# Scaling and turning x of block 3 later, and building the turned output weights of the last two pairs later

## The chip, the cores and the metric

The kernel runs on one core of a Trainium2 chip. What counts is the device time of one execution in microseconds (us), as the median of several runs; three runs of the kernel before took 1274.93 to 1278.03 us. A core has five engines, each with its own queue of instructions in a fixed order: TensorE (PE, matmuls), VectorE (DVE), ScalarE (ACT), GpSimd (POOL) and SyncE (SP, which issues DMA transfers here). Engines wait for each other through semaphores only.

## The reference

Two batches of q, k, v with 6016 rows and 256 channels go through attention over channels, and the 12032 rows that come out go through a gated feed-forward network.

```
qn = q / (norm(q, axis=1) + 1e-06);  kn = k / (norm(k, axis=1) + 1e-06)
a = softmax(kn.transpose(0, 2, 1) @ qn / tau)        # 256 x 256 per batch
x = (v @ a).reshape(12032, 256)
xn = x / sqrt(mean(x * x, axis=-1) + 1e-06) * rms_g
g = xn @ w_gate;  val = xn @ w_val                    # 256 -> 1536
out = (g / (1 + exp(-g)) * val) @ w_out               # 1536 -> 256
```

All is float32. The kernel splits each operand into a high and a low part and adds three products, so that the result keeps its accuracy.

## The kernel before, in words

The first 130 us or so load q and k and add up the scores. The rest is the feed-forward network over blocks of up to 512 rows. A block j is walked in 12 steps f = 0 to 11, one per 128 of the 1536 hidden channels. Blocks 0 and 1 use a plain form (`emit_hidden`). From block 2 on, `emit_step` forms gate and value of a step by a scheme with seven products in place of eight, for which x of the block is kept in seven combinations (`xp`) and the weights in turned form (`s_hl`, made by `build_s`). From block 4 on, the pairs of steps in `PAIRS = (2, 3, 4)` use the same scheme for the output matmuls, with output weights turned by `build_so` (lines 598 to 620).

**A step.** `emit_step` works on three values of f at once: `now` begins products 5 and 1, `mid_` adds 3 and 6, `old` adds 7, 2 and 4. The four groups of PE instructions are therefore, in order: 7 and 2 of old, 3 and 6 of mid, 5 and 1 of now, then the first half of the output matmuls of a step five steps back, product 4 of old, and the second half. Products 1, 6, 7 and 4 share one half of a PSUM bank, `u[:, 1]`: ACT copies it away between them (line 771 after product 1, line 766 after product 6), and DVE adds it up after product 7 (line 759, then 760). PE may start product 3 only when line 771 is done, product 7 only when line 766 is done, and product 4 only when line 759 is done. For even f of old, ACT then applies Silu (lines 775 and 793); for odd f, DVE multiplies (lines 778 and 787) and the result is rounded on ACT (line 692) and its low part made on POOL (line 698). The buffers `t` of lines 766 and 771 are two, those of `u` three.

**What sets the order.** The kernel runs under a manual schedule: each engine's queue is filled in the order in which Python emits the instructions. Around the steps, two tables do this. `turn0` to `turn4`, `steady` and their `_mid` forms name per block and per f what is emitted within a step (`mid`, ahead of the output matmuls) or behind it; `extra`, filled by `at(j, f, go)`, names single pieces behind the step (j, f).

**x of a block.** `emit_x` makes v @ a in PSUM, `emit_x_squares` and `emit_rr` the norm of each row, `emit_xn` (line 476, ACT) scales half a block. `emit_xT_move` transposes 32 x 32 pieces on DVE (line 511) and, after the second half, issues 16 SBUF-to-SBUF copies on SP (line 520). `emit_xT_scale` multiplies by rms_g (line 530, ACT), `emit_xT_parts` forms the combinations on POOL (lines 541 and 546), `emit_xT_round` rounds them (line 558, ACT) and makes low parts (line 560, POOL). In block 2 this is done for block 3 by `turn2` and `turn2_mid`.

**A build of output weights.** `build_so(k, 0)` adds high and low part (line 602) and forms four combinations (line 612, four instructions), all on DVE; `build_so(k, 1)` rounds them on ACT (line 618, two); `build_so(k, 2)` makes low parts on DVE (line 620, two). They share one buffer, `wk`, with each other and with the output sums of a block: the evictions of block 3 (line 940, emitted after step 4 of block 4) can start only when the last build has been read. `move_v` (line 413, DVE) transposes v of a later block.

Of the kernel before, what the change touches and what calls it, by code (L numbers as in the profile page):

```python
# [19 lines left out]
def kernel(  # L20
# [62 lines left out]
    def f32(ap):  # L83
        return ap.bitcast(F32)
# [382 lines left out]
    def emit_xn(j, h, share=False):  # L467
        px, rr = xps.pop((j, h))
        for i, t in enumerate(half_tiles(j, h)):
            if share and i == 0:  # L470
                nc.vector.tensor_scalar(
                    out=xnt[j][:, t, :], in0=px[:, i, :], scalar1=rr[:, i:i + 1], scalar2=None,
                    op0=ALU.mult,
                )
                continue
            nc.scalar.activation(
                out=xnt[j][:, t, :], in_=px[:, i, :], func=AF.Copy, scale=rr[:, i:i + 1]
            )
# [26 lines left out]
    def emit_xT_move(j, c):  # L505

        n = blocks[j][2]
        if c == 0:
            moved[j] = xn_p.tile([P, KC, A, BT, S], F32, tag="moved", name=f"xw_{j}")
        w = moved[j]  # L510
        nc.vector.transpose(
            out=w[:, c, :, :n, :].rearrange("p i t s -> p t i s"),
            in_=xnt[j][:, :n, c * P:(c + 1) * P].rearrange("p t (i r) -> p t i r", r=S),
        )
        if c < KC - 1:
            return
        x = xn_p.tile([P, KC, BN], F32, tag="xn", name=f"xnT_{j}")
        for a in range(A):
            for i in range(A):
                nc.sync.dma_start(  # L520
                    out=x[S * i:S * (i + 1), :, a * n * S:(a + 1) * n * S],
                    in_=w[S * a:S * (a + 1), :, i, :n, :].rearrange("p c t s -> p c (t s)"),
                )
        moved[j] = x
# [73 lines left out]
    def build_so(k, piece):  # L598
        p = PAIRS[k]
        if piece == 0:  # L600
            t = s_tmp["so", k] = pool["wk"].tile([P, 4, 2 * P], F32, tag="wk", name=f"wo_{k}")
            nc.vector.tensor_tensor(
                out=t[:, :2], in0=f32(wo[0][:, 2 * p:2 * p + 2]), in1=f32(wo[1][:, 2 * p:2 * p + 2]),
                op=ALU.add,
            )
            a12, a22, a11, a21 = (t[:, i, e * P:(e + 1) * P] for i in range(2) for e in range(2))
            s1, s2, s3, s4 = (t[:, 2 + i, e * P:(e + 1) * P] for i in range(2) for e in range(2))
            for o, i0, i1, op in (
                (s1, a21, a22, ALU.add), (s2, s1, a11, ALU.subtract),
                (s3, a11, a21, ALU.subtract), (s4, a12, s2, ALU.subtract),  # L610
            ):
                nc.vector.tensor_tensor(out=o, in0=i0, in1=i1, op=op)
        else:
            t = s_tmp["so", k][:, 2:].rearrange("p i n -> p (i n)")
            src = (t[:, :3 * P], t[:, 3 * P:])
            hi, lo = ([x[:, k], w[:, 2 * p + 1, P:]] for x, w in zip(so_hl, wo))
            for o, x in zip(hi, src) if piece == 1 else ():
                nc.scalar.activation(out=o, in_=x, func=AF.Copy)
            for o, x, y in zip(lo, src, hi) if piece == 2 else ():
                nc.vector.tensor_tensor(out=o, in0=x, in1=f32(y), op=ALU.subtract)  # L620
# [341 lines left out]
    with tc.manual_schedule():  # L962
# [128 lines left out]
        def at(j, f, go):  # L1091
            extra.setdefault((j, f), []).append(go)
# [43 lines left out]
        for i in (2, 3, 0, 1):  # L1136
            for p in range(NP):
                j, f = divmod(NF + at_step[p][i], NF)
# [12 lines left out]
            )  # L1151

        at(STRA - 1, 6, new_so)
        for i, k, f in ((0, 0, 10), (1, 0, 11), (2, 0, 12), (0, 1, 12), (1, 1, 13), (2, 1, 14), (0, 2, 14), (1, 2, 15)):
            at(STRA - 1 + f // NF, f % NF, lambda k=k, i=i: build_so(k, i))

        at(3, 1, lambda: inverse_norms(1))
# [31 lines left out]
        def xn(h):  # L1189
            return lambda n: emit_xn(n, h)  # L1190

        def xm(c):
            return lambda n: emit_xT_move(n, c)
# [4 lines left out]
        def of(m, go):  # L1198

            def run(j):  # L1200
                n = j + m
                if m < 0 and n < WINO or n >= NB:
                    return
                go(n)
            return run

        v0, s0, v1, s1 = (of(2, go) for go in (vm(0), vs(0), vm(1), vs(1)))
        x0, q0, r0, n0, x1, q1, r1, n1 = (of(2, go(h)) for h in range(2) for go in (x, sq, rr, xn))
# [5 lines left out]
        after = lambda m, *gos: tuple(of(m, go) for go in gos)  # L1214
# [22 lines left out]
            5: (rest,),  # L1237
            6: (s1, store),
        }
        turn4_mid = {4: (lambda j: build_so(2, 2),), 6: (x0, q0, r0), 8: (x1, q1), 9: (n1,)}  # L1240
        turn3 = {
            3: (v0,),
            4: (c0, c1, scale, s0),
# [6 lines left out]
            11: (m0, m1),  # L1250
        }
        turn3_mid = {5: (parts,), 7: (x0, q0, r0), 9: (x1, q1), 11: (n1,)}
        turn2_mid = {**turn3_mid, 0: after(1, xn(1)), 5: ()}
        turn2 = {
            **turn3,
            0: after(1, xm(0), xm(1)),
            4: (s0,),
            5: (scale,),
            6: (parts, hi, v1),
# [36 lines left out]
        for i, (j, f) in enumerate(steps + [(None, None)] * 2):  # L1296
# [5 lines left out]
            k = min(j, 5) if j is not None else None  # L1302
# [56 lines left out]
```

## Time and profile before

| what | value |
|---|---|
| median of three runs | 1277.2 us (1274.93 to 1278.03) |
| profiled execution | 1276.13 us |
| its span, first to last instruction | 1274.3 us |
| busy: PE / DVE / ACT / POOL | 99% / 69% / 68% / 63% |
| share of the chain that ended last on PE | 91% |
| PE clock granted over the span | 0.996 of full speed |

The span is what the profiler's rows cover; 1.8 us of the execution lie around it. In the timelines below a row is one instruction, or several alike in a row with their count. It gives the start from the span's beginning, how long it took, the engine, the line, what it writes and reads and in which shape. A bracket at its end says how long the engine was idle in front of it, and what it waited for.

### The profile page before, as it was taken

Reading aid. Unit: us, or ns where it says so; the run is one execution under the profiler, and the core shown is the slowest. Engines: PE = TensorE matmul, PEld = TensorE weight load, DVE = VectorE, ACT = ScalarE, POOL = GpSimd, SP = SyncE. Lnnn points to the kernel's source line nnn. Section 1 sums busy time; section 2 is a strip of 40 time slices with the busy share of each in tenths; the row PEclk is TensorE's granted clock in tenths of the full one; section 3 lists DMA queues with packets and bytes.
Section 4 is the critical chain, followed back from the end, with each engine's and each line's share of the span. In section 5 each row is a group of like instructions: output and inputs, shape, how many; then the busy total and the mean of one; then the engine's idle time right before and its main releaser. Section 6 shows DMA issues by size and latency. Waiting matters only on the chain.

```text
span 1274.3 us, 25137 instructions
## 1 busy us (share of the span) xinstructions
PE 1259.3 (99%) x9225; PEld 1199.5 (94%) x9225; DVE 884.7 (69%) x1573; ACT 869.6 (68%) x1771; POOL 803.0 (63%) x639
## 2 busy tenths in 40 slices
PE   8899999999999999999999999999999999999998
PEld 7798988999999999999999999999999999999998
DVE  5789688658667657667766666676676676676664
ACT  5577556666777687677777767767767767777654
POOL 0120245765777777777776777777777777777652
PEclk9999999999999999999999999999999999999999
DMA  8879111120221211211212202202202202101101
GB/s 286 292 239 282 50 27 42 26 42 18 46 32 24 45 25 34 41 27 34 38 23 42 36 19 47 34 18 51 34 18 51 34 18 50 30 19 30 18 1 30
DMA packets 223964, 71.77 MB, mean 56 GB/s; under 512 B 186592, under 2 KB 215392, under 8 KB 223840
## 3 DMA queue, kind: packets, MB, share of 16 engines
q1 hardware_dynamic: 223008, 68.92, 23.6%
q8 instruction: 72, 1.18, 0.4%
q10 hardware_dynamic: 832, 1.25, 0.3%
q14 instruction: 52, 0.43, 0.1%
HBM read 46.40 MB, written 12.32 MB: 46 GB/s over the span
## 4 chain that ended last, share of the span: by engine, by line
PE 91%; DMA 3%; DVE 3%; SPq 1%; ACT 1%; issue 1%; POOL 0%; POOLq 0%; DVEq 0%; ACTq 0%
PE pu L730 44%; PE po L904 26%; PE pq L730 7%; PE px L435 5%; PE s L174 4%; DMA raw<-in_k_dram 2%; PE po L854 2%; PE pg L813 1%; PE pv L813 1%; DVE wk L587 1%; SPq L520 1%; DMA raw<-in_q_dram 1%; DVE acc L198 0%; DMA wraw<-in_moe_w_out_dram 0%; DVE zh L827 0%
## 5 line engine op out<-in xcount | busy, mean ns | idle before, releaser
L730 PE MATMUL pu<-xt,w 128*128 128x256 f32 (+1 forms) x2376 | 410.7, 281 | 0.4 <-DVE zv L759 0.3
L730 PE MATMUL pu<-xt,s 128*128 128x256 f32 (+1 forms) x2376 | 366.0, 280 | 0.8 <-ACT t L766 0.8
L730 PEld LDWEIGHTS pu<-xt,w 128*128 128x128 f32 x2376 | 347.2, 189 | 13.9 <-DVE zv L759 1.0
L730 PEld LDWEIGHTS pu<-xt,s 128*128 128x128 f32 x2376 | 326.9, 188 | 13.2 <-ACT t L766 1.0
L698 POOL TENSOR_TENSOR gy<-zg,gy 128x512 fp32r<-128x512 f32 (+1 forms) x131 | 182.2, 1391 | 149.6 <-ACT gy L692 85.5
L698 POOL TENSOR_TENSOR gx<-zg,gx 128x512 fp32r<-128x512 f32 (+2 forms) x131 | 200.8, 1533 | 87.3 <-ACT gx L692 85.1
L771 ACT ACTIVATE t<-pu 128x512 f32<-128x512 f32 (+1 forms) x264 | 157.0, 595 | 99.6 <-PE pu L730 83.4
L904 PE MATMUL po<-gx,w 128*128 128x256 f32 (+1 forms) x927 | 197.4, 331 | 0.0
L766 ACT ACTIVATE t<-pu 128x256 f32<-128x256 f32 (+1 forms) x264 | 100.1, 379 | 90.4 <-PE pu L730 87.8
L759 DVE TENSOR_TENSOR zv<-pu,t 128x512 f32<-128x512 f32 (+1 forms) x132 | 89.7, 679 | 102.8 <-ACT zg L793 76.6
L778 DVE TENSOR_TENSOR zg<-zg,zv 128x768 f32<-128x768 f32 (+1 forms) x132 | 148.9, 1128 | 14.4 <-ACT t L766 0.5
L692 ACT ACTIVATE gx<-zg 128x512 fp32r<-128x512 f32 (+2 forms) x132 | 95.1, 720 | 72.2 <-DVE zg L787 36.9
L684 DVE TENSOR_TENSOR zg<-zg 128x256 f32<-128x256 f32 x228 | 96.9, 425 | 67.8 <-POOL gx L698 61.9
L904 PEld LDWEIGHTS po<-gx,w 128*128 128x128 f32 x927 | 137.1, 188 | 6.1 <-ACT os L940 0.2
L730 PE MATMUL pq<-xt,w 128*128 128x256 f32 (+1 forms) x792 | 137.3, 281 | 0.0
L787 DVE TENSOR_TENSOR zg<-pu,zg 128x256 f32<-128x256 f32 (+1 forms) x132 | 55.6, 421 | 95.3 <-PE pu L730 94.1
L759 DVE TENSOR_TENSOR zg<-pu,t 128x512 f32<-128x512 f32 (+1 forms) x132 | 89.0, 674 | 44.3 <-PE pu L730 28.7
L904 PE MATMUL po<-gy,w 128*128 128x512 f32 x414 | 118.4, 394 | 0.0
L698 POOL TENSOR_TENSOR gz<-zg,gz 128x512 fp32r<-128x512 f32 x57 | 112.8, 1979 | 0.0
L730 PEld LDWEIGHTS pq<-xt,w 128*128 128x128 f32 x792 | 112.2, 188 | 0.0
L775 ACT ACTIVATE zg<-zg 128x768 f32<-128x768 f32 (+1 forms) x132 | 109.6, 831 | 0.0
L174 PE MATMUL s<-raw 128*128 128x256 f32 x376 | 89.6, 394 | 6.8 <-DMA raw<-in_k_dram 4.5
(146 smaller groups left out, 2041.1 us busy)
## 6 DMA issues: line engine op xcount, KB each, us to landing
v<-in_v_dram SPq DMA_DIRECT2D x84, 128.0 KB, 3.8
xnT<-xw SPq DMA_DIRECT2D x336, 32.0 KB, 1.9
out_dram<-ob SPq DMA_DIRECT2D x84, 128.0 KB, 3.3
raw<-in_q_dram SPq DMA_DIRECT2D x20, 512.0 KB, 5.9
raw<-in_k_dram SPq DMA_DIRECT2D x19, 512.0 KB, 6.8
wraw<-in_moe_w_gate_dram SPq DMA_DIRECT2D x12, 256.0 KB, 4.4
wraw<-in_moe_w_val_dram SPq DMA_DIRECT2D x12, 256.0 KB, 4.9
wraw<-in_moe_w_out_dram SPq DMA_DIRECT2D x12, 256.0 KB, 5.6
```

The source lines that it names most:

```text
L174: nc.tensor.matmul(out=s_ps[b][:, c, :], lhsT=r[:, 1, t, c * P:(c + 1) * P], rhs=r[:, 0, t, :], start=(t0 + t == 0 and c == 0), stop=(t0 + ...
L435: nc.tensor.matmul(out=px[:, i, :], lhsT=w[:, c, i * P:(i + 1) * P], rhs=x[:, c, :], start=(i == 0 and c == 0 and m == 0), stop=(c == KC - ...
L684: nc.vector.tensor_tensor(out=z[:, o], in0=z[:, i0], in1=z[:, i1], op=ALU.subtract)
L692: nc.scalar.activation(out=gh, in_=hh, func=AF.Copy)
L698: engine.tensor_tensor(out=gl, in0=hh, in1=f32(gh), op=ALU.subtract)
L730: nc.tensor.matmul(out=out, lhsT=wm[wi], rhs=xm[xi], start=(start and q == 0), stop=(q == 2), skip_group_check=True,)
L759: nc.vector.tensor_tensor(out=z[:, 1:], in0=u, in1=t[:, :2], op=ALU.add)
L766: nc.scalar.activation(out=mt[:, 0], in_=mu[:, 1], func=AF.Copy)
L771: nc.scalar.activation(out=nt[:, 1:], in_=nu, func=AF.Copy)
L775: nc.scalar.activation(out=zg[:, 1:], in_=zg[:, 1:], func=AF.Silu)
L778: nc.vector.tensor_tensor(out=zg[:, 1:], in0=zg[:, 1:], in1=z, op=ALU.mult)
L904: nc.tensor.matmul(out=acc[b][:, o:o + g.shape[-1]], lhsT=w, rhs=g, start=first, stop=True, skip_group_check=True,)
```

## The change

Five lines of the tables change. For block 3, the scaling of the second half of x (`xn(1)`) is emitted within step 1 of block 2 instead of step 0, and the two transposes with the copies (`xm(0)`, `xm(1)`) behind step 2 instead of step 0. The builds of output weights for pairs 3 and 4 (k = 1 and 2) move by one or two steps; two of their pieces go from behind a step to within it.

```diff
         at(STRA - 1, 6, new_so)
-        for i, k, f in ((0, 0, 10), (1, 0, 11), (2, 0, 12), (0, 1, 12), (1, 1, 13), (2, 1, 14), (0, 2, 14), (1, 2, 15)):
+        for i, k, f in ((0, 0, 10), (1, 0, 11), (2, 0, 12), (0, 1, 13), (1, 1, 14), (0, 2, 15)):
             at(STRA - 1 + f // NF, f % NF, lambda k=k, i=i: build_so(k, i))
...
-        turn4_mid = {4: (lambda j: build_so(2, 2),), 6: (x0, q0, r0), 8: (x1, q1), 9: (n1,)}
+        turn4_mid = {3: (lambda j: build_so(1, 2),), 4: (lambda j: build_so(2, 1), lambda j: build_so(2, 2)), 6: (x0, q0, r0), 8: (x1, q1), 9: (n1,)}
...
-        turn2_mid = {**turn3_mid, 0: after(1, xn(1)), 5: ()}
+        turn2_mid = {**turn3_mid, 1: after(1, xn(1)), 5: ()}
         turn2 = {
             **turn3,
-            0: after(1, xm(0), xm(1)),
+            2: after(1, xm(0), xm(1)),
```

On ACT at the start of block 2 (`t` and `pu` belong to the steps, `xn` and `px` to block 3, `ob` is the output of block 1), before:

```order
L771 ACTIVATE t_0_1929<-pu_0_1928 128x512
L476 ACTIVATE xn_1862<-px_1_1813,rr_1_1914 128x256 x2
L878 ACTIVATE ob_1965<-po_1_1436 128x512
L878 ACTIVATE ob_1965<-po_1_1437 128x512
L766 ACTIVATE t_0_1929<-pu_0_1928 128x256
L771 ACTIVATE t_1_1976<-pu_1_1975 128x512
L766 ACTIVATE t_1_1976<-pu_1_1975 128x256
```

and with the change:

```order
L771 ACTIVATE t_0_1929<-pu_0_1928 128x512
L878 ACTIVATE ob_1943<-po_1_1436 128x512
L878 ACTIVATE ob_1943<-po_1_1437 128x512
L766 ACTIVATE t_0_1929<-pu_0_1928 128x256
L771 ACTIVATE t_1_1954<-pu_1_1953 128x512
L476 ACTIVATE xn_1862<-px_1_1813,rr_1_1914 128x256 x2
L766 ACTIVATE t_1_1954<-pu_1_1953 128x256
```

The two scalings went behind the eviction of block 1 and the first two copies of the steps. On DVE at the same place (`xw` are the transposed pieces, `wk` here a build of gate and value weights, line 587):

```order
-L511 STREAM_TRANSPOSE xw_1939<-xn_1862 128x4x4x32 x2
-L759 TENSOR_TENSOR zg_0_2000<-pu_0_1928,t_0_1929 128x512
-L760 TENSOR_TENSOR zg_0_2000<-pq_0_1996,t_0_1929 128x256
+L759 TENSOR_TENSOR zg_0_1980<-pu_0_1928,t_0_1929 128x512
+L760 TENSOR_TENSOR zg_0_1980<-pq_0_1976,t_0_1929 128x256
+L511 STREAM_TRANSPOSE xw_2002<-xn_1862 128x4x4x32 x2
 L587 TENSOR_TENSOR wk_1889<-wk_1889 128x256 x4
```

The transposes went from in front of the first sums to behind them. On DVE at the seam of blocks 3 and 4, from the sum of f = 11 of block 3 on (`wo` is the build's buffer, `so` and `w` its results), before:

```order
L602 TENSOR_TENSOR wo_3166<-w_97,w_98 128x512
L612 TENSOR_TENSOR wo_3166<-wo_3166 128x128 x4
L759 TENSOR_TENSOR zv_11_3183<-pu_11_3058,t_11_3059 128x512
...
L413 STREAM_TRANSPOSE vw_0_3217<-v_2944 128x4x2x32 x2
L759 TENSOR_TENSOR zg_0_3235<-pu_0_3127,t_0_3128 128x512
L760 TENSOR_TENSOR zg_0_3235<-pq_0_3231,t_0_3128 128x256
L620 TENSOR_TENSOR so_2833<-wo_3166,so_2832 128x384
L620 TENSOR_TENSOR w_98<-wo_3166,w_97 128x128
L602 TENSOR_TENSOR wo_3265<-w_97,w_98 128x512
L612 TENSOR_TENSOR wo_3265<-wo_3265 128x128 x4
L759 TENSOR_TENSOR zv_1_3282<-pu_1_3172,t_1_3173 128x512
```

and with the change:

```order
L413 STREAM_TRANSPOSE vw_0_3211<-v_2944 128x4x2x32 x2
L602 TENSOR_TENSOR wo_3218<-w_97,w_98 128x512
L612 TENSOR_TENSOR wo_3218<-wo_3218 128x128 x4
L759 TENSOR_TENSOR zg_0_3233<-pu_0_3127,t_0_3128 128x512
...
L778 TENSOR_TENSOR zg_0_3233<-zg_0_3233,zv_1_3274 128x768
L620 TENSOR_TENSOR so_2833<-wo_3218,so_2832 128x384
L620 TENSOR_TENSOR w_98<-wo_3218,w_97 128x128
L787 TENSOR_TENSOR zg_0_3233<-pu_1_3166,zg_0_3233 128x256
L413 STREAM_TRANSPOSE vw_1_3312<-v_2944 128x4x2x32 x2
L602 TENSOR_TENSOR wo_3315<-w_97,w_98 128x512
L612 TENSOR_TENSOR wo_3315<-wo_3315 128x128 x4
L759 TENSOR_TENSOR zg_2_3330<-pu_2_3224,t_2_3225 128x512
```

Lines 602 and 612 of each of the two builds now stand between the transposes of line 413 and the sum of an even step.

## Rows read from the trace of the kernel before

**Rows 1.** The page: busy time, share of the span and count of each engine

```profile
PE 1259.3 (99%) x9225; PEld 1199.5 (94%) x9225; DVE 884.7 (69%) x1573; ACT 869.6 (68%) x1771; POOL 803.0 (63%) x639
```

**Rows 2.** Timeline of PE, first steps of block 2: start us, us, what, idle before

```profile
208.79 0.62 PE L730 MATMUL pu<-xt,s 128*128 128x256 f32 x3 [0.84 <-ACT t L766]
...
219.70 0.63 PE L730 MATMUL pu<-xt,w 128*128 128x256 f32 x3
...
224.74 0.51 PE L730 MATMUL pu<-xt,s 128*128 128x256 f32 x3
```

**Rows 3.** Timeline of ACT, same stretch

```profile
206.65 0.84 ACT L476 ACTIVATE xn<-px,rr 128x256 f32<-128x256 f32 x2 [1.07 <-POOL rr L464]
207.38 1.08 ACT L878 ACTIVATE ob<-po 128x512 f32<-128x512 f32 x2
208.33 0.40 ACT L766 ACTIVATE t<-pu 128x256 f32<-128x256 f32 x1
...
221.69 1.32 ACT L530 ACTIVATE xnT<-xnT,g_sb 128x512 f32<-128x512 f32 x2
```

**Rows 4.** Timeline of DVE, same stretch

```profile
207.57 1.30 DVE L511 STREAM_TRANSPOSE xw<-xn 128x512 f32<-128x512 f32 x2 [0.94 <-POOL rr L464]
209.54 0.69 DVE L759 TENSOR_TENSOR zg<-pu,t 128x512 f32<-128x512 f32 x1 [0.66 <-PE pu L730]
...
218.96 0.68 DVE L759 TENSOR_TENSOR zv<-pu,t 128x512 f32<-128x512 f32 x1
```

**Rows 5.** SP's queue in its timeline, and the landing of these copies from the tile's view

```profile
209.01 10.74 SPq L520 DMA_DIRECT2D xnT<-xw  x16
...
DMA to landing us min/median/max: 1.8/1.9/3.1
```

**Rows 6.** Timeline of PE, steps 2 to 5 of block 4

```profile
304.74 0.51 PE L730 MATMUL pu<-xt,s 128*128 128x256 f32 x3
...
307.57 0.52 PE L730 MATMUL pu<-xt,w 128*128 128x256 f32 x3
...
308.62 0.51 PE L730 MATMUL pu<-xt,s 128*128 128x256 f32 x3
...
311.88 0.62 PE L730 MATMUL pu<-xt,w 128*128 128x256 f32 x3 [0.26 <-DVE zv L759]
...
313.03 0.51 PE L730 MATMUL pu<-xt,s 128*128 128x256 f32 x3
...
319.06 0.86 PE L904 MATMUL po<-gx,w 128*128 128x512 f32 x3
```

**Rows 7.** Timeline of DVE, steps 0 to 3 of block 4

```profile
299.88 0.69 DVE L602 TENSOR_TENSOR wo<-w,w 128x512 f32<-128x512 f32 x1
300.61 1.02 DVE L612 TENSOR_TENSOR wo<-wo 128x128 f32<-128x128 f32 x4
...
304.66 0.76 DVE L413 STREAM_TRANSPOSE vw<-v 128x256 f32<-128x256 f32 x2
...
309.15 2.07 DVE L612 TENSOR_TENSOR wo<-wo 128x128 f32<-128x128 f32 x4
```

**Rows 8.** Timeline of POOL, steps 2 to 4 of block 4

```profile
305.23 1.30 POOL L698 TENSOR_TENSOR gx<-zg,gx 128x512 fp32r<-128x512 f32 x1 [2.33 <-ACT gx L692]
306.49 1.29 POOL L398 TENSOR_TENSOR vt<-vw,vt 128x512 fp32r<-128x512 f32 x1
309.38 1.29 POOL L698 TENSOR_TENSOR gy<-zg,gy 128x512 fp32r<-128x512 f32 x1 [1.60 <-ACT gy L692]
...
315.30 1.29 POOL L541 TENSOR_TENSOR xp<-xnT 128x512 f32<-128x512 f32 x1
316.67 1.75 POOL L546 TENSOR_TENSOR xp<-xnT,xp 128x256 f32<-128x256 f32 x2
```

**Rows 9.** Timeline of ACT, step 4 of block 4: the evictions of block 3

```profile
318.28 1.09 ACT L940 ACTIVATE os<-po 128x512 f32<-128x512 f32 x2
```

## The prediction

> **What bounds the kernel now.** The busy line of the page comes first: TensorE (PE) works for 1259.3 of 1274.3 us [rows 1]. What an edit of the order can win is therefore idle time of PE, and what it can lose is new idle time. The second view is PE's timeline around the two places that the change touches: the start of block 2 (about 203 to 225 us) and the seam of blocks 3 and 4 (about 297 to 325 us). From 205.1 us on, every bracketed idle time of PE lies in these places, so they hold all there is to win. In the first, PE sits idle 0.84 us in front of product 7 of f = 0, waiting for the copy of line 766 on ACT [rows 2]. In the second, product 4 of f = 1 waits 0.26 us for the sum of line 759 on DVE, and that step takes 313.03 - 308.62 = 4.41 us where the step ahead of it takes 3.88 [rows 6]: a stall of 0.53 in all. Both together are 1.37 us.
>
> What a step tolerates is read from the same rows. Product 4 overwrites the half bank that line 759 reads, so line 759 has to be over by then: 307.57 - 304.74 = 2.83 us after the step's first product [rows 6]. Last come the timelines of DVE, ACT, POOL and SP in these places [rows 3 to 5] [rows 7 to 9], for what is queued around those waits.
>
> **Place 1: x of block 3.** On ACT the two scalings (line 476, 0.84 us) stood between the first copy of f = 0 and the eviction of block 1 (line 878, 1.08 us), and line 766 behind them [rows 3]. Now the eviction goes first and the scalings fall into a later wait. Line 766 then starts about 0.84 earlier, at about 207.4, when product 6 has just ended; product 7 finds it done at its natural 207.95. Gain at this point: 0.84.
>
> The two transposes (line 511) move too. Before, they ran from 207.57 for 1.30 us while DVE had to wait for PE anyway [rows 4]. Now they stand behind the sums of f = 0, inside a stretch in which DVE goes without a gap from the sum at 209.54 to that of f = 3, which starts at 218.96 and ends about 219.64; PE's product 4 at 219.70 starts just behind that end [rows 2, 4]. So DVE, not PE, sets the pace there. The stretch starts 0.94 earlier (209.54 to about 208.6) and is 1.23 longer (two transposes, overlapping by 0.07): the sum of f = 3 ends 0.29 later, and product 4 with it. The 0.84 is spent again within four steps. **Place 1: +0.3.** Bounds: -0.84 if DVE had slack I don't see; +1.5 if the next item bites.
>
> That item is SP and the scale. The 16 copies of line 520 take 10.74 us to issue, and a copy lands 1.9 us after its issue (3.1 at most) [rows 5]. The transposes now end near 210.85 and not 208.87, so the last copy lands near 223.0. The scale of line 530, at 221.69 before [rows 3], waits to about 223.1 and ends near 224.4. Behind it on ACT is the copy of line 766 that product 7 of f = 5 needs, at 224.74 + 0.29 = 225.03 [rows 2]. Some 0.6 us are left for a copy of 0.4: nothing, with little margin. The store of block 1 now goes ahead of these copies on SP, which is idle then: nothing. POOL's order does not change here; its pieces of x run a microsecond later, where PE has no use for them before block 3 begins, and I cost that at nothing.
>
> **Place 2: turned output weights of the last two pairs.** A build is line 602 and four of line 612 on DVE, two copies of line 618 on ACT, two subtractions of line 620 on DVE. Alone, lines 602 and 612 take 0.69 + 1.02 [rows 7]. Before, each such pair stood behind an even step's sums, where DVE has time. Now each stands behind an odd step's last product and the transposes of line 413, directly ahead of an even step's line 759.
>
> Step 2 (f = 0 finishing): line 413 ends at 304.66 + 0.76 = 305.42 [rows 7]. POOL began a subtraction of 1.30 us at 305.23 and has the next (1.29) queued behind it [rows 8]. What such company costs: the four of line 612 took 1.02 alone and 2.07 when a POOL subtraction began at 309.38, just after their first [rows 7, 8]; the extra 1.05 is the rest of POOL's instruction. So line 602 waits to 306.53 and ends near 307.1; POOL takes its next, delayed to about 308.25; the first of line 612 follows at 308.4, and the other three, with POOL idle, end near 309.1. Line 759 needs 0.69 more: 309.75. Product 4 was due at 307.57: **2.2 us of new stall.** Without POOL it would be 305.42 + 1.71 + 0.69 - 307.57 = 0.25.
>
> The rule behind that row speaks against this change. The Trainium skill (SBUF — State Buffer, Who interferes with whom) says that a VectorE instruction with two SBUF inputs and a GpSimd instruction that reads SBUF lock each other out, and that the later one blocks until the first is done. By it step 2 costs the 2.2; if the two engines slowed each other without such a lock, it would cost something nearer the 0.25. The trace agrees with the lock: 2.07 against 1.02.
>
> Step 3: with the old builds gone, its 0.53 of stall goes: **-0.53**. Here ACT copies the second pair's build only after line 793, so its subtractions (line 620) stand between lines 778 and 787, behind POOL's subtraction of gy.
>
> Step 4, on a clock 2.2 later: by the same bookkeeping line 787 ends near 315.5 and line 413 near 316.25. Then line 602 waits for the end of POOL's gx (316.5), ends near 317.05, and the parts of line 612 pass one by one between line 541 (1.29) and the two of line 546 (1.75 together) [rows 8]: 318.4, 319.4, 320.3, 320.5. Line 759 ends near 321.1. Product 4 was due at 308.62 + 2.2 + 3.88 + 2.83 = 317.53: **3.6 us of new stall.** Alone: about 0.4.
>
> Step 5: line 618 now follows line 775 on ACT, and line 620 follows line 618; the evictions of line 940 write the same wk buffer, so they wait for line 620. Their first was at 318.28, and the output matmuls that need it went at 319.06 [rows 6, 9]. Now they come about 3.4 us behind the sum of f = 2, the matmuls are due 3.2 behind it, and each eviction takes 0.55: **0.8 us.** Bounds 0 and 1.5. After that, step 6 holds px and takes up what ACT and POOL are late.
>
> **The sum.** Place 2: 2.2 - 0.53 + 3.6 + 0.8 = +6.1 (alone, without POOL: about 0.25 - 0.53 + 0.4 + 0.7 = +0.8). Place 1: +0.3. Together +6.4 us, to 1282.5 on the profiled execution's 1276.13. That execution lies 1.1 below the median of the three runs, 1277.2; on the median it is **1283.6 us**. Nothing later can give it back, since PE has no other idle time. About 0.3% (3.8 us) is what a measurement of this kernel can tell from no change.
>
> **Rivals.**
> 1. The builds pass POOL more lightly than I count: line 602 gets in first, or the parts of line 612 pass together. For it: the two engines' turns hang on offsets of 0.2 us (305.42 against 305.23). Against: line 612's 2.07 at 309.15 shows a full wait. Then the sum lies between +0.8 and +3.7, 1278.0 to 1280.9: no change that can be told. Chance 0.27.
> 2. The change does what it looks like: both stalls go and DVE takes the builds in its idle time. It decides at one point: if line 759 of step 2 ends before 307.57, the builds fitted. Place 1 gives -0.84 and place 2 -0.53: 1275.8, not slower. For it: DVE is busy only 69% [rows 1]. Against: from the end of line 413 there are 307.57 - 305.42 = 2.15 us up to that point, and the builds and the sum need 1.71 + 0.69 = 2.4 even alone [rows 6, 7]. Chance 0.06.
> 3. It adds up further: the late scale of block 3 delays product 7 too, or POOL's pieces of block 5 push the step 4 builds back by another two instructions (2 to 3 us): 1286 to 1289. Chance 0.05.
> That the change does nothing is excluded: the order of DVE and ACT differs.
>
> **The numbers.** Forecast 0.62, its own range +3.8 to +8.5, 1281.0 to 1285.7. Rival 1, and all but a third of rival 2, are no change: 0.27 + 0.04 = 0.31. Slower: 0.62 + 0.05 = 0.67. Faster by 3.8 us would need more than the two stalls hold; 0.02 of rival 2 is kept for what I don't see. The range goes from 1277.0 to 1286.5: its low end lies 1 us under rival 1, as far as one run of the kernel lies from the next, and it leaves out rival 2, most of rival 3 and the rim of both, under 0.2 in all.
>
> **What would show it.** Right: PE's 0.84 in front of product 7 gone, but products 4 of f = 1 to 3 in block 2 waiting for line 759; in block 4 product 4 of f = 0 idle some 2 us and of f = 2 some 3 to 4 us, both released by line 759; line 612's four instructions taking over 2 us; steps from 6 on unchanged. Wrong: if the two groups of lines 602 and 612 take about 1.7 us each, the lock did not bite and rival 1 holds; if PE shows no idle time at 307.6, rival 2 does.

## The result, and the profile after

The changed kernel took 1281.34 us (median of five runs, 1280.47 to 1281.98) against 1276.32 us for the kernel before (five runs, 1274.17 to 1278.03). The ratio is 1.0051 with a 95% interval of 1.0037 to 1.0065, or 4.7 to 8.3 us: slower by more than the 0.3% that can be told from no change. The two medians lie 5.0 us apart, inside that interval. The prediction was 1283.6 us, +6.4, range 1277.0 to 1286.5.

On the page of the changed kernel the counts are those of [rows 1] and hardly any busy time was added: PE is busy for 1260.3 us against 1259.3. The profiled span is 1279.5 us against 1274.3, so most of the 5.2 is idle time of PE. The timeline of PE in the changed kernel, first at the start of block 2 and then at the seam of blocks 3 and 4 (start us, us, what, idle before and who ended it; the rows at 206.29, 223.13, 303.14, 310.20, 314.74, 321.24 and 325.92 are product 7, the first of a step):

```profile
206.29 0.53 PE L730 MATMUL pu<-xt,s 128*128 128x256 f32 x3
...
214.51 0.62 PE L730 MATMUL pu<-xt,w 128*128 128x256 f32 x3 [0.22 <-DVE zg L759]
...
223.13 0.51 PE L730 MATMUL pu<-xt,s 128*128 128x256 f32 x3
...
303.14 0.51 PE L730 MATMUL pu<-xt,s 128*128 128x256 f32 x3
...
308.16 0.96 PE L730 MATMUL pu<-xt,w 128*128 128x256 f32 x3 [2.02 <-DVE zg L759]
...
310.20 0.84 PE L730 MATMUL pu<-xt,s 128*128 128x256 f32 x3
...
314.74 0.51 PE L730 MATMUL pu<-xt,s 128*128 128x256 f32 x3
...
320.08 0.63 PE L730 MATMUL pu<-xt,w 128*128 128x256 f32 x3 [2.35 <-DVE zg L759]
...
321.24 0.51 PE L730 MATMUL pu<-xt,s 128*128 128x256 f32 x3
...
324.05 0.98 PE L904 MATMUL po<-gx,w 128*128 128x512 f32 x3 [0.34 <-ACT os L940]
...
325.92 0.51 PE L730 MATMUL pu<-xt,s 128*128 128x256 f32 x3
```

**Place 1.** The 0.84 of idle time in front of product 7 of f = 0 is gone, and from there to product 7 of f = 5 it now takes 223.13 - 206.29 = 16.84 us against 224.74 - 208.79 = 15.95 [rows 2]: 0.89 longer, and where PE waited on the way, at 214.51, it was for line 759. Net +0.05.

**Place 2.** Steps 2 to 5 last 7.06, 4.54, 6.50 and 4.68 us. Before they lasted 3.88, 4.41 [rows 6], 3.89 and 3.89, the last two by these rows of PE's timeline before:

```profile
316.92 0.51 PE L730 MATMUL pu<-xt,s 128*128 128x256 f32 x3
...
320.81 0.52 PE L730 MATMUL pu<-xt,s 128*128 128x256 f32 x3
```

The difference is 3.18 + 0.13 + 2.61 + 0.79 = +6.71. The span grew by only 5.2, because this execution reached place 1 some 1.7 us sooner (product 7 of f = 0 would have come at 208.79 - 0.84 = 207.95 before, and came at 206.29). Nothing that the change touches runs there: the same product stands at 207.21 in the profile of the experiment with the x part alone.

What held product 4 at 308.16 and 320.08 is seen on DVE and POOL. The timeline of DVE of the changed kernel:

```profile
303.75 1.73 DVE L602 TENSOR_TENSOR wo<-w,w 128x512 f32<-128x512 f32 x1
305.52 1.98 DVE L612 TENSOR_TENSOR wo<-wo 128x128 f32<-128x128 f32 x4
307.42 0.68 DVE L759 TENSOR_TENSOR zg<-pu,t 128x512 f32<-128x512 f32 x1
...
315.27 0.65 DVE L602 TENSOR_TENSOR wo<-w,w 128x512 f32<-128x512 f32 x1
315.95 3.48 DVE L612 TENSOR_TENSOR wo<-wo 128x128 f32<-128x128 f32 x4
```

and of POOL in the same stretch:

```profile
303.64 1.29 POOL L698 TENSOR_TENSOR gx<-zg,gx 128x512 fp32r<-128x512 f32 x1 [2.35 <-ACT gx L692]
304.89 1.73 POOL L398 TENSOR_TENSOR vt<-vw,vt 128x512 fp32r<-128x512 f32 x1
...
315.24 1.83 POOL L698 TENSOR_TENSOR gx<-zg,gx 128x512 fp32r<-128x512 f32 x1 [2.54 <-ACT gx L692]
317.03 1.32 POOL L541 TENSOR_TENSOR xp<-xnT 128x512 f32<-128x512 f32 x1
318.43 1.66 POOL L546 TENSOR_TENSOR xp<-xnT,xp 128x256 f32<-128x256 f32 x2
```

Line 602 took 1.73 us where it took 0.69 alone [rows 7]: POOL's gx ran until 304.93. POOL's next instruction took 1.73 and not 1.29, as line 602 got in between the two; then the first of line 612 waited for that one, and its other three passed freely. Lines 602 and 612 and these instructions of POOL read nothing that the other writes, and no bracket stands in front of the rows: the waits lie inside their lengths. So semaphores are not the only way in which one engine waited for another in this kernel. In step 4 line 602 and POOL's gx begin 0.03 us apart. Starts so close don't tell who came first, the lengths do: 0.65 is line 602's own time, so it went first, and gx lost 0.54 (1.83 against 1.29). In step 2, where it began 0.11 us behind gx, it had waited. Of the four of line 612 three then waited for one instruction of POOL each (gx, line 541 and the first of line 546), and one passed: 3.48 us against 1.02 alone.

A part of the +6.71 was not idle time. The busy time of the engines behind the first of the two idle times (stretch: length, busy of PE, PEld, DVE, ACT, POOL with counts, granted clock, DMA share, GB/s):

```profile
308.10:310.20 2.10, 2.04 (x7) 1.75 (x7) 0.33 (x2) 1.65 (x4) 0.00 (x0) 0.53 0.00 0
310.20:312.00 1.80, 1.80 (x11) 1.80 (x10) 0.85 (x2) 1.08 (x3) 0.59 (x1) 0.60 0.00 0
```

After its 2.02 us of idle time PE ran at the lower of its two levels, 1.2 GHz, in nearly all of the first stretch and most of the second; after the 2.35 us it stayed at 2.4 GHz (granted clock 1.00 from 320.00 to 321.20). From product 4 to the next product 7 it took 310.20 - 308.16 = 2.04 in step 2, against 321.24 - 320.08 = 1.16 in step 4, behind an idle time too but at 2.4 GHz: 0.88 for the clock. In step 3 it is 0.13 + 0.53 = 0.66 more, as the stall of the old builds is gone there. Together 1.54.

Step 5 lost its 0.79 on ACT. The timeline of ACT, then of DVE:

```profile
321.70 0.51 ACT L618 ACTIVATE so<-wo 128x384 fp32r<-128x384 f32 x1
...
322.58 0.94 ACT L558 ACTIVATE xt<-xnT 128x256 fp32r<-128x256 f32 x2
323.41 1.08 ACT L940 ACTIVATE os<-po 128x512 f32<-128x512 f32 x2
```

```profile
322.73 0.28 DVE L620 TENSOR_TENSOR w<-wo,w 128x128 fp32r<-128x128 f32 x1
```

Line 620 was over at 323.01, but the evictions of line 940 began at 323.41, straight behind line 558 and with no idle time in front: they stood in ACT's queue. The two of line 618, in front of line 558 now, took 0.62 of it (321.70 to 322.32). The output matmuls came some 0.6 later by that; the other 0.2 is product 5, which waited for line 793, also behind line 618.

### The profile page after: what moved, and what is told of

The parts are those of the page before. It is cut to its first block, busy times and chain, and to the rows that moved or that the text cites. A ratio compares the mean times of both kernels' runs of the same rounds, so it can differ in the third digit from the quotient of the medians.

```text
span 1279.5 us, 25135 instructions
## 1 busy us (share of the span) xinstructions
PE 1260.3 (99%) x9225; PEld 1199.7 (94%) x9225; DVE 885.0 (69%) x1573; ACT 870.0 (68%) x1771; POOL 803.9 (63%) x639
## 3 DMA queue, kind: packets, MB, share of 16 engines
q8 instruction: 72, 1.18, 0.4%
## 4 chain that ended last, share of the span: by engine, by line
PE 88%; DVE 5%; DMA 3%; SPq 1%; issue 1%; ACT 1%; POOL 0%; POOLq 0%; DVEq 0%; ACTq 0%
PE pu L730 43%; PE po L904 26%; PE pq L730 7%; PE px L435 5%; PE s L174 2%; PE po L854 2%; DMA raw<-in_k_dram 2%; DVE acc L198 2%; PE pg L813 1%; PE pv L813 1%; SPq L520 1%; DVE wk L587 1%; DMA raw<-in_q_dram 0%; DMA xnT<-xw 0%; DVE wo L612 0%
## 5 line engine op out<-in xcount | busy, mean ns | idle before, releaser
L174 PE MATMUL s<-raw 128*128 128x256 f32 x376 | 86.5, 383 | 6.5 <-DMA raw<-in_k_dram 4.2
```

The lines of the kernel that those rows point to most:

```text
L174: nc.tensor.matmul(out=s_ps[b][:, c, :], lhsT=r[:, 1, t, c * P:(c + 1) * P], rhs=r[:, 0, t, :], start=(t0 + t == 0 and c == 0), stop=(t0 + ...
```

## The experiments

Each ratio below is to the kernel before as it was timed beside that experiment (medians 1274.04 to 1275.01 us over 21 to 27 runs), not to the 1276.32 us above. Lengths of steps are read in one profile of each kernel.

**The x part alone.** Against the kernel before:

```diff
-        turn2_mid = {**turn3_mid, 0: after(1, xn(1)), 5: ()}
+        turn2_mid = {**turn3_mid, 1: after(1, xn(1)), 5: ()}
...
-            0: after(1, xm(0), xm(1)),
+            2: after(1, xm(0), xm(1)),
```

> The change to x of block 3 alone; the builds of output weights stand as before. Theory (builds wait for POOL at the seam, x is about neutral): within 1 us of the kernel before; PE's 0.84 in front of product 7 in block 2 gone, its product 4 of f = 1 to 3 waiting for line 759 instead, and the seam as before with its stall of 0.5 us. Rival (x and its late scale carry the loss): about 5 us slower than before.

Measured: 1275.33 us, ratio 1.0004 (0.9993 to 1.0015): no difference. PE's timeline:

```profile
207.21 0.55 PE L730 MATMUL pu<-xt,s 128*128 128x256 f32 x3
...
224.07 0.52 PE L730 MATMUL pu<-xt,s 128*128 128x256 f32 x3
```

The 0.84 in front of product 7 is gone, and 224.07 - 207.21 = 16.86 is 0.91 longer than before: net +0.07. The gain is won and spent again within a few steps, through line 759; PE waited 0.22 us for it at 215.45.

**The builds alone.** The kernel before with the two lines of the change on `build_so`:

```diff
-        for i, k, f in ((0, 0, 10), (1, 0, 11), (2, 0, 12), (0, 1, 12), (1, 1, 13), (2, 1, 14), (0, 2, 14), (1, 2, 15)):
+        for i, k, f in ((0, 0, 10), (1, 0, 11), (2, 0, 12), (0, 1, 13), (1, 1, 14), (0, 2, 15)):
...
-        turn4_mid = {4: (lambda j: build_so(2, 2),), 6: (x0, q0, r0), 8: (x1, q1), 9: (n1,)}
+        turn4_mid = {3: (lambda j: build_so(1, 2),), 4: (lambda j: build_so(2, 1), lambda j: build_so(2, 2)), 6: (x0, q0, r0), 8: (x1, q1), 9: (n1,)}
```

> The later builds alone; x of block 3 as before. Theory: all of the loss is here, 5 to 7 us slower than before; in block 4 product 4 of f = 0 idle about 2 us and of f = 2 about 2.4 us, both released by line 759. Rival (x carries the loss): within 1 us of before.

Measured: 1280.04 us, ratio 1.0043 (1.0028 to 1.0058), 5.5 us. The builds are all of the loss that can be told. PE's timeline:

```profile
302.54 0.51 PE L730 MATMUL pu<-xt,s 128*128 128x256 f32 x3
...
307.55 0.63 PE L730 MATMUL pu<-xt,w 128*128 128x256 f32 x3 [2.02 <-DVE zg L759]
...
308.71 0.51 PE L730 MATMUL pu<-xt,s 128*128 128x256 f32 x3
...
312.58 0.51 PE L730 MATMUL pu<-xt,s 128*128 128x256 f32 x3
...
318.60 0.63 PE L730 MATMUL pu<-xt,w 128*128 128x256 f32 x3 [3.04 <-DVE zg L759]
...
319.77 0.51 PE L730 MATMUL pu<-xt,s 128*128 128x256 f32 x3
...
324.44 0.51 PE L730 MATMUL pu<-xt,s 128*128 128x256 f32 x3
```

Steps 2 to 5 take 6.17, 3.87, 7.19 and 4.67: +2.29 - 0.54 + 3.30 + 0.78 = +5.83. Here the whole place ran at 2.4 GHz, after idle times of 2.02 and 3.04 too (columns as above):

```profile
307.00:325.00 18.00, 14.10 (x92) 12.39 (x93) 14.14 (x23) 11.61 (x25) 9.70 (x8) 1.00 0.01 3
```

PE's idle time in step 4 was expected at about 2.4 us and was 3.04. DVE's timeline of steps 3 and 4 has the reason:

```profile
311.33 1.65 DVE L620 TENSOR_TENSOR so<-wo,so 128x384 fp32r<-128x384 f32 x1
...
314.12 0.81 DVE L602 TENSOR_TENSOR wo<-w,w 128x512 f32<-128x512 f32 x1
314.96 2.99 DVE L612 TENSOR_TENSOR wo<-wo 128x128 f32<-128x128 f32 x4
```

Here line 620 waited for POOL's gy, and line 602, 1.54 us into the step, came while gx was running (313.07 to 314.37) and waited for its end. The last of line 612 got through behind the second of line 546's two. In the changed kernel line 620 took 0.54 alone, line 602 came 0.53 us into the step and went ahead of gx, and the last of line 612 got through behind the first of line 546: that is the 0.7 us between 3.30 and 2.61. The second profile of the changed kernel has the same 0.65 and 3.48 for the two lines. There line 620 took 1.64, but line 787 behind it still had to wait for PE, which ran step 3 at the lower clock in both profiles. So it seems to be the clock of step 3 that moved line 602 ahead of gx; this is read from three traces and was not tried apart.

**The builds where they are, without the second input from SBUF.** Against the changed kernel; lines 602 and 612 become transposes of their first input, of the same shape (their lines below are one higher from 613 on):

```diff
-            nc.vector.tensor_tensor(
-                out=t[:, :2], in0=f32(wo[0][:, 2 * p:2 * p + 2]), in1=f32(wo[1][:, 2 * p:2 * p + 2]),
-                op=ALU.add,
+            nc.vector.transpose(
+                out=t[:, :2].rearrange("p i (a r) -> p i a r", r=32),
+                in_=f32(wo[0][:, 2 * p:2 * p + 2]).rearrange("p i (a r) -> p i a r", r=32),
...
-                nc.vector.tensor_tensor(out=o, in0=i0, in1=i1, op=op)
+                nc.vector.transpose(out=o.rearrange("p (a r) -> p a r", r=32), in_=i0.rearrange("p (a r) -> p a r", r=32))
```

> The changed kernel, its order kept, with line 602 and the four of line 612 made transposes of one SBUF operand in the same shapes; this leaves out the sums and differences that turn the output weights, so the output is another. Theory (the builds wait for POOL because both read two SBUF operands): each build takes about 1.7 us, product 4 of f = 0 idle 0.2 to 0.4 us and of f = 2 at most 0.5, no half clock at the seam, the whole within 1.5 us of the kernel before. Rival (the place behind the transposes of line 413 is too late whatever POOL does): idle times of 2 us stay, and 4 to 7 us over before.

Measured: 1276.08 us, ratio 1.0009 (0.9998 to 1.0019): the loss is all but gone, with the builds still at the changed places. The timeline of DVE, step 2 and then step 4:

```profile
303.32 0.67 DVE L602 STREAM_TRANSPOSE wo<-w 128x512 f32<-128x512 f32 x1
304.03 1.04 DVE L613 STREAM_TRANSPOSE wo<-wo 128x128 f32<-128x128 f32 x4
...
309.49 1.65 DVE L621 TENSOR_TENSOR so<-wo,so 128x384 fp32r<-128x384 f32 x1
```

with POOL's timeline beside it (gx stood at 303.21 and took 1.30), and PE's in step 4:

```profile
304.47 1.30 POOL L398 TENSOR_TENSOR vt<-vw,vt 128x512 fp32r<-128x512 f32 x1
```

```profile
310.74 0.51 PE L731 MATMUL pu<-xt,s 128*128 128x256 f32 x3
...
314.65 0.62 PE L731 MATMUL pu<-xt,w 128*128 128x256 f32 x3 [0.92 <-DVE zg L760]
...
315.81 0.52 PE L731 MATMUL pu<-xt,s 128*128 128x256 f32 x3
```

The same two POOL instructions stand beside the builds as in the changed kernel, and now neither side is lengthened. Steps 2 to 5 take 4.14, 3.88, 5.07 and 4.67: +0.26 - 0.53 + 1.18 + 0.78 = +1.7. What lines 602 and 612 pay to POOL is thus 5.83 - 1.7 = some 4.1 of the 5.83. What the place itself costs, without it, stays: 0.26 in step 2, where the prediction said 0.25 alone. The 0.92 us of idle time in step 4 is more than the 0.5 expected at most, and the 1.18 more than the prediction's 0.4. Line 621 (620 of the other kernels), still a subtraction with two inputs from SBUF, took 1.65 behind POOL's gy in step 3 against 0.54 by itself. From there to the sum of line 760, over at 314.60, DVE has hardly any idle time, so these 1.1 us came through to product 4. By this reading the lock between the two engines is worth some 5.2 of the 5.83; a run without that wait was not made. Step 5 kept its 0.78 without the sums of lines 602 and 612, as ACT's order is the same.

The Trainium skill (SBUF — State Buffer, Who interferes with whom) says that a VectorE instruction with two SBUF inputs contends with GpSimd's reads of SBUF, and one with a single SBUF input does not. This trace agrees on both: 1.73 for the sum against 0.67 for the transpose, beside the same work of POOL.

**The last pair alone.** The kernel before, with the pieces of pair 4 alone where the change puts them:

```diff
-        for i, k, f in ((0, 0, 10), (1, 0, 11), (2, 0, 12), (0, 1, 12), (1, 1, 13), (2, 1, 14), (0, 2, 14), (1, 2, 15)):
+        for i, k, f in ((0, 0, 10), (1, 0, 11), (2, 0, 12), (0, 1, 12), (1, 1, 13), (2, 1, 14), (0, 2, 15)):
...
-        turn4_mid = {4: (lambda j: build_so(2, 2),), 6: (x0, q0, r0), 8: (x1, q1), 9: (n1,)}
+        turn4_mid = {4: (lambda j: build_so(2, 1), lambda j: build_so(2, 2)), 6: (x0, q0, r0), 8: (x1, q1), 9: (n1,)}
```

> Only the last pair is built later (as in the changed kernel); pair 3 is built as before and x is as before. Theory: step 2 of block 4 keeps its 3.9 us; step 3 loses its 0.5 us of stall; step 4 gains 2.5 to 3.6 us of idle time in front of product 4 and step 5 0.8: 3 to 4 us over before, and up to 1.6 more if the clock is halved after that idle time. Rival (both builds must move for the loss, through the shared buffer): within 1 us of before.

Measured: 1278.03 us, ratio 1.0034 (1.0023 to 1.0044). PE's timeline:

```profile
309.42 0.51 PE L730 MATMUL pu<-xt,s 128*128 128x256 f32 x3
...
315.44 0.62 PE L730 MATMUL pu<-xt,w 128*128 128x256 f32 x3 [3.03 <-DVE zg L759]
316.60 0.68 PE L730 MATMUL pu<-xt,s 128*128 128x256 f32 x3
```

Step 4 takes 7.18, +3.29, as in the experiment with both builds: the two builds pay separately, and step 4's price does not need the delay from step 2. Line 602 began 0.11 us behind gx here and waited (1.73), and the four of line 612 took 2.99 again. Step 5 takes 5.40 here (316.60 to 322.00), 0.73 more than with both builds, with the lower clock from 316.79 on.

**The later pieces of both builds earlier.** Rounding (line 618) and low parts (line 620) a step or more ahead of where they stood. Against the kernel before:

```diff
-        for i, k, f in ((0, 0, 10), (1, 0, 11), (2, 0, 12), (0, 1, 12), (1, 1, 13), (2, 1, 14), (0, 2, 14), (1, 2, 15)):
+        for i, k, f in ((0, 0, 10), (1, 0, 11), (2, 0, 12), (0, 1, 12), (1, 1, 12), (0, 2, 14), (1, 2, 14)):
...
-        turn4_mid = {4: (lambda j: build_so(2, 2),), 6: (x0, q0, r0), 8: (x1, q1), 9: (n1,)}
+        turn4_mid = {1: (lambda j: build_so(1, 2),), 3: (lambda j: build_so(2, 2),), 6: (x0, q0, r0), 8: (x1, q1), 9: (n1,)}
```

> The kernel before, with the builds moved the other way: lines 602 and 612 stay behind even steps, the copies of line 618 follow them a step earlier than before, and the subtractions of line 620 go into the odd step, behind line 778; x as before. Theory (a build costs nothing where it stands behind an even step's sums): the 0.53 us of stall in step 3 of block 4 goes and nothing takes its place, steps 0 to 5 at 3.9 us each, 0.5 us under before. Rival (line 620 between lines 778 and 787 delays the odd step as well): steps 1 and 3 over 4.1 us, no gain.

Measured: 1275.62 us, ratio 1.0004 (0.9994 to 1.0015). The 0.53 in step 3 is gone (3.88), but step 4 takes 5.33, +1.44. DVE's timeline:

```profile
309.07 1.65 DVE L620 TENSOR_TENSOR so<-wo,so 128x384 fp32r<-128x384 f32 x1
```

Now the two subtractions of line 620 (1.65 and 1.36) met POOL's gy and gx, which began at 308.37 and 310.26, and line 787, queued behind them, let product 5 of f = 4 wait 1.19 us. Neither the theory nor its rival had the loss in step 4.

**The later pieces of pair 3 alone earlier.** Pair 4 as in the kernel before:

```diff
+        for i, k, f in ((0, 0, 10), (1, 0, 11), (2, 0, 12), (0, 1, 12), (1, 1, 12), (0, 2, 14), (1, 2, 15)):
...
+        turn4_mid = {1: (lambda j: build_so(1, 2),), 4: (lambda j: build_so(2, 2),), 6: (x0, q0, r0), 8: (x1, q1), 9: (n1,)}
```

> The kernel before with pair 3 alone built earlier: the copies of line 618 behind step 0 of block 4, the subtractions of line 620 within step 1; pair 4 and x as before. Theory (line 620 between lines 778 and 787 is harmless in step 1, where POOL is idle at that time, and cost step 3 dear, where POOL was busy): steps 1 to 5 of block 4 at 3.88 to 3.93 us each, the 0.53 of step 3 gone, 0.5 us under before and too little to be timed. Rival: what goes in step 3 comes back in another step, as in the run with both pairs early.

Measured: 1274.78 us, ratio 1.0008 (0.9999 to 1.0017). Only 0.08 of the 0.53 in step 3 went (4.33). The timeline of DVE:

```profile
307.98 2.12 DVE L612 TENSOR_TENSOR wo<-wo 128x128 f32<-128x128 f32 x4
```

In the experiment above, the same four took 1.02, from 306.13 on. There ACT rounded the build (line 618) ahead of gy, so POOL's gy came only when line 612 was over. Here, as in the kernel before, nothing stood ahead of gy on ACT; POOL's gy began at 308.64, 0.66 us after line 612, and got in between its parts, as before [rows 7, 8]. Whether the two met went with what a third engine did first.

**The x part with a piece of a weight build on POOL.** As the x part alone, and for one pair line 587 runs on POOL:

```diff
-                nc.vector.tensor_tensor(out=t[:, o], in0=t[:, i0], in1=t[:, i1], op=op)
+                (nc.gpsimd if p == 4 else nc.vector).tensor_tensor(out=t[:, o], in0=t[:, i0], in1=t[:, i1], op=op)
```

> The change to x alone, and the four differences of line 587 for pair 4 made on POOL, which is idle then, in place of DVE. Theory (DVE sets the pace in the first steps of block 2, and the moved transposes take there what ACT gives): with 1.7 us less on DVE, product 4 of f = 1 to 3 no longer waits for line 759; the four steps behind product 7 of f = 0 take 11.6 to 12.0 us in place of 13.0, about 1 us under the change to x alone. Rival (ACT or PE sets the pace there): the steps stay within 0.3 us.

Measured: 1273.18 us, ratio 0.9992 (0.9979 to 1.0005). The four steps from product 7 of f = 0 on take 12.21 us together, against 12.98 with the x part alone: DVE did set the pace there, though the gain is less than expected (11.6 to 12.0). But then the late scale of block 3 came out, in ACT's timeline:

```profile
219.50 1.34 ACT L530 ACTIVATE xnT<-xnT,g_sb 128x512 f32<-128x512 f32 x2 [1.66 <-DMA xnT<-xw]
```

ACT waited 1.66 us for the copies of line 520 and product 7 of f = 5 waited 0.19 for line 766 behind it.

**The pieces together.** The x part with line 587 on POOL, and the later pieces of both builds earlier:

> Both of these together: x later, line 587 of pair 4 on POOL, and the builds as in the kernel with early copies. Theory: 1.3 to 1.8 us under the kernel before by the lengths of the steps, about 0.1%, which the timed runs can hardly tell from no change. Rival: no shorter steps than in the kernel before.

Measured: 1275.88 us, ratio 1.0010 (1.0000 to 1.0019): the gain did not come, as step 4 of block 4 takes 5.34, like without the x part. With the pieces of pair 3 alone in their place:

> The same, with x of block 3 later and line 587 of pair 4 on POOL. Theory: the steps of block 2 as in the run with x and POOL (about 0.1 us under before in all, since the late scale takes back what DVE gives), the seam 0.5 us under before: 0.6 us in all, no change that can be timed. Rival: over 1 us under before by the lengths of the steps.

Measured: 1272.99 us, ratio 0.9999 (0.9989 to 1.0010); step 3 of block 4 takes 4.36, so the 0.5 expected at the seam did not come either. No version that was tried is faster than the kernel before by an amount that can be told.

**The changed kernel once more,** for its profile:

> The changed kernel once more, for its profile. Theory: product 4 idle 2.0 us (f = 0) and 2.3 to 3.1 us (f = 2) of block 4 again. Whether PE's clock is halved after the first of them, as in its first profile, or not, as in the run with the builds alone, is open: if the idle time alone sets it, it is halved again.

Measured: 1283.63 us, a single run. PE's timeline and, under it, two stretches with their granted clock (columns as above):

```profile
310.00 0.62 PE L730 MATMUL pu<-xt,w 128*128 128x256 f32 x3 [2.02 <-DVE zg L759]
...
321.91 1.01 PE L730 MATMUL pu<-xt,w 128*128 128x256 f32 x3 [2.37 <-DVE zg L759]
```

```profile
311.20:314.60 3.40, 3.40 (x18) 3.40 (x17) 2.50 (x4) 2.30 (x6) 1.35 (x1) 0.51 0.00 0
321.40:325.00 3.60, 3.09 (x11) 2.81 (x12) 1.67 (x5) 2.70 (x7) 0.61 (x2) 0.53 0.02 5
```

The idle times are the same to 0.02 us as in the first profile; the lower clock came behind both and not behind one.

## Why the prediction was right

The terms of the sum, beside what the runs gave (us):

| term | predicted | x or builds alone | the change |
|---|---|---|---|
| place 1, x of block 3 | +0.3 | +0.07 | +0.05 |
| step 2: builds behind POOL | +2.2 | +2.29 | +2.30 |
| step 3: old builds gone | -0.53 | -0.54 | -0.53 |
| step 4: builds behind POOL | +3.6 | +3.30 | +2.61 |
| step 5: evictions of block 3 | +0.8 | +0.78 | +0.79 |
| lower clock after the idle time | none | none | +1.54 |
| sum | +6.4 | +5.9 | +6.8 |

- **Step 2** came as worked out, instruction by instruction. The changed kernel ran 304.74 - 303.14 = 1.60 earlier there, and the prediction's instants less 1.60 are: line 602 over at 305.5 (303.75 + 1.73 = 305.48), line 759 over at 308.15 (308.10, and product 4 at 308.16).
- **Step 4** was right in kind and mis-sized. With the builds alone line 602 was over 2.35 us into the step (314.93 - 312.58), just as predicted (317.05 behind a step that begins at 308.62 + 2.2 + 3.88 = 314.70); the four of line 612 then took 2.99 where the prediction has 317.05 to 320.5, so it was 3.30 and not 3.6. In the changed kernel the step "line 602 waits for the end of POOL's gx" failed: line 602 went first (0.65), line 620 was not late behind gy (0.54), and it was 2.61.
- **Step 5** hit its size by a wait that the prediction did not name: not line 620 held the evictions, but ACT's own queue with line 618 in front. The agreement of 0.79 with 0.8 is in part luck.
- **Place 1** was right in kind: the 0.84 is won and spent on DVE. Its size, 0.89 in place of 1.1, is off by two tenths. "Nothing, with little margin" for the scale held: line 530 stood at 221.20, 222.8 on the clock of before, and no product waited. Where line 587 had left DVE and the steps were 0.8 us shorter, it bit, by 0.19.
- **Not foreseen:** the lower clock behind an idle time of PE. The prediction costed a stall at its own length; here it cost 1.54 more. Where the builds ran alone, the clock stayed up and the loss was still 5.5 us, so the verdict does not hang on it. That the sum came out at +6.8 beside +6.4 is in part luck too: the clock stands against what step 4 fell short.
- **Rival 1** (builds pass POOL lightly, +0.8 to +3.7): one half of its condition came, line 602 got in first in step 4, but the parts of line 612 waited all the same (1.98 and 3.48), and the interval of 4.7 to 8.3 lies above it. The run with transposes took away most of the wait, and there the sum was +1.7. **Rival 2** falls at the point it named: line 759 of step 2 ended at 308.10, 2.1 us behind its deadline of 307.57 - 1.60 = 305.97. **Rival 3** did not come: product 7 of f = 5 in block 2 did not wait, the builds of step 4 waited for no more of POOL's instructions than were counted, and from step 6 on the steps are those of before.
- "PE has no other idle time" overlooked 0.38 us at 1265.81, where line 854 waits for POOL's line 698. The changed kernel has the same 0.38 at 1270.92, so nothing hung on it.
- The total: the median of before is 1276.32 over five runs and not 1277.2, so the same +6.4 would lead to 1282.7; 1281.34 was measured. The ratio's middle is 6.5 us, its interval 4.7 to 8.3.

## What to carry to other kernels

Before an operation is moved into a gap, look up what the other engine of a locked pair does there. Each of a chain of short VectorE instructions with two SBUF inputs can pay for an instruction of POOL: two of the five of a build did in step 2, three in step 4, so 1.7 us of work took 3.7 to 4.1. What counts is not their work but how many of POOL's instructions fall between. Such waits make a row longer and leave no idle time in front of it, so look for them in the lengths. Price it at the reader: the latest instant at which the sum may end, 2.83 us after the step's first product, told gain from loss here. And a table of turns is a three-engine matter: whether DVE and POOL met went with a copy on ACT, ahead of POOL's input or not, and the copies of line 618 ahead of the evictions cost step 5 its 0.6.

## What was not expected of the hardware

PE's clock after a stall. After 2.02 us of idle time PE ran at 1.2 GHz in the changed kernel, after 2.35 at 2.4; in its second profile it fell after both (2.02 and 2.37); with the last pair alone it fell after 3.03; with the builds alone it fell after neither 2.02 nor 3.04. So how long PE was idle does not settle it alone, and the same idle time can cost 1.5 us more in one execution than in another. Nor did the clock always fall at once: in the second profile and with the last pair alone PE had been back at work for more than 1.1 us at 2.4 GHz (granted clock 1.00 from 310.00 to 311.20 and from 315.40 to 316.60). The Trainium skill (TensorE: Matmul & The Clock Gate, What's actually happening) says that the hardware's monitoring runs freely and is not started anew by a kernel; the runs above do not contradict it, and none of them shows it.
